# A first chunk with an order of its own, in an mLSTM cell followed by a cosine-gated feed-forward layer

## The chip, the cores and the metric

The kernel runs on one core of a Trainium2 chip. The metric is the device time of one execution in microseconds (us), lower being better. Where several executions of a kernel are timed, their median is given with the lowest and the highest; one further execution was taken with the hardware profiler, and all rows shown come from that one.

The core has five engines, each with its own queue that it works off in order: TensorE (PE in the profile, with its weight loads as PEld), VectorE (DVE), ScalarE (ACT), GpSimd (POOL) and SyncE (SP), which here only issues DMAs. A waiting instruction holds up all that stand behind it in its queue.

## The reference

```python
# q, k, v, o_gate: (4, 8, 768, 40); i_gate, f_gate: (4, 8, 768)
for t in range(S):
    m_new = np.maximum(f[t] + m, i[t])
    f_stab, i_stab = np.exp(f[t] + m - m_new), np.exp(i[t] - m_new)
    m = m_new
    C = f_stab * C + i_stab * outer(v[t], k[t])      # (B, H, 40, 40)
    n = f_stab * n + i_stab * k[t]
    y[t] = sigmoid(o[t]) * (C @ q[t]) / max(abs(n . q[t]), 1)
x = y as (3072, 320)                                 # heads side by side
h = x @ w_in                                         # (3072, 2048)
out = (h * cos(h)) @ w_out                           # (3072, 320)
```

The weights w_in (320 x 2048) and w_out (2048 x 320) arrive as 64-bit floats and are turned into 32-bit floats on the chip.

## The kernel before

**Tiling.** The sequence of 768 is cut into 6 chunks (c) of 128 steps. A chunk of one batch element (b = 0 to 3) with all 8 heads is a cell, n = 4c + b. Within a cell the recurrence is done as matrix products: scores (L490), a decay matrix E that is masked (`decay_exponents`, L396, POOL), exponentiated (`decay`, L410, ACT) and multiplied into the scores (`weigh`, L496, DVE), then values (`values`, L506 to L525, PE) into vt. Between cells the state st[b] is faded (`fade`, L588, POOL), its increment is computed (`seam`, L605) and added (`state`, L627, DVE). `normalize_turned` (L534 to L546) makes x of vt and of the o gate, which `turn_gate` (L468) has turned.

**Two parts beside each other.** While the cells of chunk c + 1 are computed, the feed-forward layer of chunk c runs (`both_parts`, called for each c and b). Its 2048 hidden columns are cut into 16 blocks of 128; a half (c, b, i) handles two of them, f2 = 2b + i. The steps of a half, in the order of data: up-products into two PSUM banks (`Up`, L645 and L651, PE), rounding (`near`, L659, ACT), the remainder (`rest`, L662, DVE), sine (`sin`, L667, ACT), gate (`gate`, L671, DVE), which frees the PSUM bank for the next half's up-products. One half later come the down-products with w_out: in chunk 0 plainly (`down`, L683), in later chunks with 7 products for 8 (`products`, L761), for which POOL makes sums of w_out in chunk 1 (`weight_sums`, L707 to L710). I write 1.0 for b = 1, i = 0 of chunk 0, and round b for its two halves.

**The weights are made in chunk 0.** A piece of w_in (512 columns of one of two row blocks, or the piece of the last 64 rows, w_in_l) or of w_out (two blocks) is loaded as bits by SP, then taken apart on ACT (`take_apart`, two activations, L150 and L152), joined on DVE (`put_together`, L157, L159, L161), and the last addition is done on POOL (L162). `to_float32` is both. Block f of w_in (four hidden blocks) has three pieces; it is needed from half f.0 = (b = f, i = 0) on. Piece p of w_out is needed by the down-products of half p.

**What sets the order.** It is written out by hand: the program's order on each engine is the order of the calls, `first_cells` and then the halves. Loads are issued by SP in the order of their calls too, and wait there until their buffer is free. Tiles come from pools: the bits of w_in from four buffers, those of w_out from three, E from three, G (the decays of the state, multiplied onto q by `scale_q`, L472) from two. `raws` holds q and k as loaded for two cells; `turn_blocks` (L463) turns them for one cell, `low_dimensions` (L455) copies their last 8 columns, and `clear_low` (L448) fills the second pair with zeros before its first use. `warm` (L830) issues products of zeros. `sin_next` loads ACT's table for the sine ahead of need.

In chunk 0, POOL's order in half 0.0 is: qG, the mask of E for cell 5, the two fills of `clear_low`, the addition of w_out's first piece, the end of `normalize_turned`, the four operations of `fade`.

Of the kernel before, what the change touches and what calls it, by code (L numbers as in the profile page):

```python
# [11 lines left out]
FP = mybir.dt.float32  # L12
# [4 lines left out]
OP = mybir.AluOpType  # L17
# [12 lines left out]
def kernel(  # L30
# [153 lines left out]

    tab = const.tile([128, NC, 4, BH], FP, name="tab")
    R = NC - 1
# [91 lines left out]
    def gates_keep(pg, pd):  # L278
        nc.scalar.copy(out=tab[:, 1:NC, 0:2], in_=pg)
        nc.scalar.copy(out=tab[:, 1:R, 3], in_=pd)  # L280

# [174 lines left out]

    def turn_blocks(n):
        m = n // 2 % 2
        qkT[n] = [p1.tile([128, HP, C], FP, name=f"t{i}", tag=f"t{i}") for i in range(2)]
        for i, w in enumerate("qk"):  # L460
            x = 32 + n % 2 * (WR // 2)
            src = raws[w][m][:, x:x + WR // 2].rearrange("q (p a d) -> q p a d", a=C // 32, d=D)
            nc.vector.transpose(out=qkT[n][i].rearrange("q p (t a) -> q p a t", t=32), in_=src[:, :, :, 0:32])  # L463
# [118 lines left out]
    def fade(n):  # L582

        if B <= n < N - B:
            c, b = divmod(n, B)
            for j, r, s, w in halves(n):
                d = tab[r, c, 3, ts(b, H)].rearrange("p (a j) -> p a j", j=2)[:, :, j]
                nc.gpsimd.tensor_tensor(out=s, in0=s, in1=d.unsqueeze(2).to_broadcast([D, HP, w.stop - w.start]), op=OP.mult)  # L588

# [237 lines left out]
    def warm(k, bank=None):  # L827

        for _ in range(k):
            nc.tensor.matmul(bank or pw, nil, nil.unsqueeze(1).to_broadcast([128, HP, 128]), start=True, stop=True)  # L830

    def first_cells():
        nc.vector.memset(nil, 0.0)
# [71 lines left out]
        outs.append((0, weights_out(0)))  # L905
        load_o(1)
        weigh(2)
        decay_exponents(3)
# [13 lines left out]
        pieces.extend(weights_in(1))  # L922
        load_E(B + 1)
        outs.append((1, weights_out(1)))
# [21 lines left out]
        odd_values(B)  # L946
        scale_q(B)

    spot = const.tile([1, 1], FP, name="spot")
# [6 lines left out]
    def next_out():  # L956
        p, piece = outs.pop(0)
        to_float32(*piece)
        if p + 3 < NF // 2:
            outs.append((p + 3, weights_out(p + 3)))  # L960

    def both_parts(c, b):
# [3 lines left out]
        for i in range(2):  # L966
            f2 = 2 * b + i
            up = Up(c, f2, c > 0 and i == 1)
            if cell and i == 0:
                scores(n)  # L970
                if c == 0 and b == 0:

                    warm(8, psum_o())
            if cell and i == 1:
# [6 lines left out]
            if i == 0:  # L981
                if cell:
                    weigh(n)
                    if n + 1 < N:
                        decay_exponents(n + 1)
                    if n == B:
                        clear_low()
                for e in range(2):
                    up.sin(e)
                    up.gate(e)  # L990
                if (c, b) == (0, 0):
                    turn_blocks(n + 1)
                if c > 0:
                    sums(c, f2)
                if c == 1 and b > 0:
                    weight_sums(f2)
                if b == 0 and 0 < c < NC - 1:
                    sigmoid(c + 1)

                if c == 0 and b > 0 and pieces:  # L1000
                    to_float32(*pieces.pop(0))
                if c == 0:
                    next_out()
                if (c, b) == (0, 0):
                    sigmoid(1)
                elif cell and n + 1 < N:
                    decay(n + 1)
            else:
                if pieces:
                    to_float32(*pieces.pop(0))  # L1010
# [5 lines left out]
                if c > 0:  # L1016
                    sums(c, f2)
                if c == 1:
                    weight_sums(f2)
                if n == B + 1:  # L1020
                    low_dimensions(n + 1)
                if (c, b) == (0, 0):
                    decay(n + 1)
                    sin_next()
                while pieces:
                    to_float32(*pieces.pop(0))
                if cell and n + 1 < N:
# [3 lines left out]
            if cell and i == 0:  # L1031
# [12 lines left out]
                if b == B - 2 and c + 2 < NC:  # L1044
                    load_o(c + 2)
                if c == 0 and pieces:
                    to_float32(*pieces.pop(0))
                sin_next()
# [3 lines left out]
            if i == 1:  # L1052
                if c == 0 and b + 2 < B:
                    pieces.extend(weights_in(b + 2))
                    load_two((n + 3) // 2 * 2)
                    load_E(n + 3)
                if cell and n + 1 < N:
                    if (c, b) != (0, 0):
                        turn_blocks(n + 1)
                    scale_q(n + 1)  # L1060
                if c == 0:
                    next_out()

    pieces, outs = [], []
    with tc.manual_schedule():
        first_cells()
        for c in range(NC):
            for b in range(B):
                both_parts(c, b)
        run(made_of[NC - 1], 14)  # L1070
# [33 lines left out]
```

## Time and profile before

| | us |
|---|---|
| median of 3 executions (lowest to highest) | 547.65 (546.9 to 549.5) |
| the profiled execution | 544.86 |
| its span in the profile | 543.0 |
| busy in the span: PE | 516.1 |
| busy: DVE | 423.9 |
| busy: ACT | 283.4 |
| busy: POOL | 262.6 |
| first up-products of chunk 0 to those of chunk 1 (40.1 to 139.1) | 99.0 |

The page gives the busy time of each engine, the span in 40 equal slices, the groups of equal instructions with the idle time ahead of them and what ended it, and the chain of work that ended last. L numbers are lines of the kernel. In a row of a group, the tiles stand as out<-in, then partitions x elements and the type, then how often; behind the bar the busy time in all (us), the mean of one (ns), and the idle time of the engine just ahead of them with its releaser. Rows of the timeline have start and duration in us instead, and merge equal instructions in a row. A row's PE time is that of instructions whose ends are modelled, so that start to start is the better measure. The granted clock is the share of full speed at which TensorE was allowed to run.

### The profile page before, as it was taken

What the parts mean: (1) busy time and instruction counts of PE and PEld (TensorE: products, weight loads), DVE (VectorE), ACT (ScalarE), POOL (GpSimd) and SP (SyncE); (2) the same over time, 40 slices, a digit from 0 to 9 for tenths busy, and PEclk for the clock granted to TensorE, in tenths of its full rate; (3) what the DMA queues carried; (4) which work ended last, traced back from release to release, by engine and by line L of the source; (5) the groups of instructions that cost most, each with busy time, mean ns of one, the idle gap of its engine ahead of it and who ended that gap; (6) DMA issues with size and microseconds to landing.
All of it is one profiled execution on the core that took longest, in us unless ns stands there. A gap on an engine that the chain in (4) does not pass through costs nothing.

```text
span 543.0 us, 10536 instructions
## 1 busy us (share of the span) xinstructions
PE 516.1 (95%) x3842; PEld 349.4 (64%) x3842; DVE 423.9 (78%) x906; ACT 283.4 (52%) x539; POOL 262.6 (48%) x446
## 2 busy tenths in 40 slices
PE   7999498989989999999999999999999999999996
PEld 4884264545556767657767757767757767575756
DVE  5897879997876887887878887887888878664636
ACT  2879767746565537546527546436546533221321
POOL 7542866465467777744553545554424432221211
PEclk9969699999999999999999999999999999999999
DMA  9998997998327539229449319338420000010001
GB/s 136 222 207 199 277 195 227 192 235 172 44 94 166 63 97 193 51 75 185 45 103 179 46 72 198 47 105 174 44 82 18 1 5 6 2 49 1 0 1 48
DMA packets 98051, 57.81 MB, mean 106 GB/s; under 512 B 62336, under 2 KB 90080, under 8 KB 98000
## 3 DMA queue, kind: packets, MB, share of 16 engines
q1 hardware_dynamic: 96528, 55.64, 48.9%
q0 software_dynamic: 1424, 1.49, 1.2%
q8 instruction: 30, 0.49, 0.4%
q14 instruction: 21, 0.17, 0.1%
q10 hardware_dynamic: 48, 0.02, 0.0%
HBM read 51.71 MB, written 4.11 MB: 103 GB/s over the span
## 4 chain that ended last, share of the span: by engine, by line
PE 69%; DVE 11%; ACT 6%; issue 5%; POOL 4%; SPq 3%; DMA 1%; ACTq 0%; DVEq 0%; POOLq 0%
PE pup L645 25%; PE acc L761 23%; PE pup L651 8%; PE po L683 3%; PE late L761 2%; PE ps L490 2%; DVE n L662 2%; PE vt L525 2%; PE vt L516 1%; ACT E L410 1%; DVE g L671 1%; PE pu L605 1%; SPq L327 1%; POOL w_out_sb L162 1%; DVE t L463 1%
## 5 line engine op out<-in xcount | busy, mean ns | idle before, releaser
L645 PE MATMUL pup<-xT,w_in_sb 128*128 128x512 f32 x384 | 176.1, 601 | 5.0 <-DVE g L671 5.0
L659 ACT ACTIVATE n<-pup 128x512 int32<-128x512 f32 x96 | 53.9, 596 | 207.0 <-PE pup L651 146.6
L662 DVE SCALAR_TENSOR_TENSOR n<-pup,n 128x512 f32<-128x512 f32 x96 | 63.2, 687 | 85.1 <-ACT n L659 83.5
L645 PEld LDWEIGHTS pup<-xT,w_in_sb 128*128 128x128 f32 x384 | 69.8, 190 | 91.7 <-issue 78.7
L725 POOL TENSOR_TENSOR D<-g 128x128 f32<-128x128 f32 x40 | 19.6, 490 | 150.1 <-DVE g L671 136.0
L667 ACT ACTIVATE n<-n 128x512 f32<-128x512 f32 x96 | 59.5, 632 | 16.4 <-DVE n L662 16.4
L671 DVE SCALAR_TENSOR_TENSOR g<-pup,n 128x512 f32<-128x512 f32 x96 | 62.2, 685 | 1.8 <-ACT n L667 0.2
L761 PE MATMUL acc<-w_out_sb,g 128*128 128x160 f32 x320 | 58.5, 304 | 0.0
L761 PE MATMUL acc<-T,g 128*128 128x160 f32 x320 | 57.8, 300 | 0.0
L651 PE MATMUL pup<-xT,w_in_l 64*128 64x512 f32 x192 | 54.3, 641 | 0.0
L761 PEld LDWEIGHTS acc<-w_out_sb,g 128*128 128x128 f32 x320 | 47.8, 190 | 5.4 <-issue 3.9
L761 PEld LDWEIGHTS acc<-T,g 128*128 128x128 f32 x320 | 48.2, 190 | 3.1 <-issue 2.7
L410 ACT ACTIVATE E<-E,tab 128x128 f32<-128x128 f32 x160 | 49.1, 391 | 0.3
L683 PE MATMUL po<-w_out_sb,g 128*128 128x320 f32 x128 | 39.5, 465 | 9.0 <-POOL w_out_sb L162 8.9
L683 PEld LDWEIGHTS po<-w_out_sb,g 128*128 128x128 f32 x128 | 25.3, 203 | 23.0 <-POOL w_out_sb L162 10.6
L761 PE MATMUL acc<-T,S 128*128 128x160 f32 x160 | 35.0, 300 | 1.9 <-POOL T L709 1.9
L546 POOL TENSOR_TENSOR yt<-yt,db 128x128 f32<-128x128 f32 x20 | 11.1, 557 | 50.4 <-DVE db L541 50.4
L396 POOL TENSOR_SCALAR_AFFINE_SELECT E<-E 128x1024 f32<-128x1024 f32 x22 | 24.5, 1113 | 19.2 <-DMA E<-M_d 14.5
L490 PEld LDWEIGHTS ps<-t,t 40*128 40x128 f32 x384 | 24.9, 188 | 10.9 <-issue 7.9
L496 DVE TENSOR_TENSOR E<-ps,E 128x512 f32<-128x512 f32 x48 | 30.7, 681 | 0.0
L472 POOL TENSOR_TENSOR qG<-t,G 128x512 f32<-128x512 f32 x20 | 25.4, 1271 | 9.4 <-DVE t L463 9.1
L651 PEld LDWEIGHTS pup<-xT,w_in_l 64*128 64x128 f32 x192 | 14.6, 184 | 23.4 <-issue 19.9
(178 smaller groups left out, 935.1 us busy)
## 6 DMA issues: line engine op xcount, KB each, us to landing
E<-M_d SPq DMA_DIRECT2D x22, 512.0 KB
qr<-in_q_dram SPq DMA_DIRECT2D x36, 160.0 KB
kr<-in_k_dram SPq DMA_DIRECT2D x36, 160.0 KB
G<-G_d SPq DMA_DIRECT2D x20, 256.0 KB
bits<-in_moe_w_out_dram SPq DMA_DIRECT2D x8, 640.0 KB
bits<-in_moe_w_in_dram SPq DMA_DIRECT2D x32, 128.0 KB
out_dram<-o_sb SPq DMA_DIRECT2D x24, 160.0 KB
o<-in_o_gate_dram SPq DMA_DIRECT2D x40, 80.0 KB
```

Source lines behind the costliest of these rows:

```text
L410: nc.scalar.activation(out=Es[n][:, h], in_=Es[n][:, h], func=AF.Exp, scale=-1.0, bias=tab[:, c, 0, g:g + 1])
L472: nc.gpsimd.tensor_tensor(out=qG, in0=qkT[n][0], in1=Gs[n], op=OP.mult)
L490: nc.tensor.matmul(ps[j][:, p], kT[r, p], qT[r, p], start=True, stop=True)
L496: nc.vector.tensor_tensor(out=w, in0=pss[n][j], in1=w, op=OP.mult)
L645: nc.tensor.matmul(pu, w_in_sb[:, i, ts(2 * f2 + e, 128)], x(i), start=(i == 0 and not low_first), stop=(i == NK - 1 and low_first))
L651: nc.tensor.matmul(pu, w_in_l[r, f2], x(NK, r), start=low_first, stop=not low_first)
L659: nc.scalar.activation(out=self.n[e], in_=self.pu[e], func=AF.Copy, bias=0.25)
L662: nc.vector.scalar_tensor_tensor(out=self.n[e].bitcast(FP), in0=self.pu[e], scalar=0.25, in1=self.n[e], op0=OP.add, op1=OP.subtract)
L667: nc.scalar.activation(out=r, in_=r, func=AF.Sin, scale=TWO_PI_DOWN)
L671: nc.vector.scalar_tensor_tensor(out=g, in0=self.pu[e], scalar=TWO_PI, in1=self.n[e].bitcast(FP), op0=OP.mult, op1=OP.mult)
L683: nc.tensor.matmul(po[c][b], gs[c, f][:, ts(b, C)], w_out_sb[:, f], start=(f == 0), stop=(f == NF - 1))
L761: nc.tensor.matmul(a, lhs, rhs, start=start, stop=stop)
```

## The change

Chunk 0 gets a function of its own, `first_parts`, in place of `both_parts`, from which the cases for chunk 0 are taken out. Its order differs from before in these points:

- in half 0.0 the addition of w_out's first piece stands ahead of the mask of E, and `clear_low` has gone to the end of `first_cells`; the second piece of ACT's w_in work stands ahead of the sigmoid;
- in halves 1.1 and 2.1 the gates stand ahead of the join of w_in_l; in 1.0 and 2.0 one join of w_in stands ahead of the gates; POOL adds w_out ahead of qG and of the mask; `turn_blocks` is split in two, with the join of w_out between q and k;
- the take-aparts on ACT are put into other places, most of them ahead of `near` of the next half, and w_in's pieces are loaded one by one (`more`), with the q and k of cells 6 and 7 ahead of the first of them; the load of E for cell 5 is issued ahead of w_in's second block;
- after the first down-products come 20 products of zeros added to the same banks (`hold`);
- `fade` is one operation on all 128 partitions and 384 columns instead of four on 40 partitions, with its factors in a tile of their own (`fades`), filled by two copies on 64 partitions each (`gates_keep`); this holds for all chunks. In chunk 0 it stands ahead of `normalize_turned`.

```diff
-    tab = const.tile([128, NC, 4, BH], FP, name="tab")
+    tab = const.tile([128, NC, 2, BH], FP, name="tab")
+    fades = const.tile([128, NC, BH // 2], FP, name="fades")
...
     def gates_keep(pg, pd):
         nc.scalar.copy(out=tab[:, 1:NC, 0:2], in_=pg)
-        nc.scalar.copy(out=tab[:, 1:R, 3], in_=pd)
+        for j in range(2):
+            r = slice(64 * j, 64 * j + 64)
+            nc.scalar.copy(out=fades[r, 1:R], in_=pd[r].rearrange("q c (g j) -> q c g j", j=2)[:, :, :, j])
...
     def fade(n):
...
-            for j, r, s, w in halves(n):
-                d = tab[r, c, 3, ts(b, H)].rearrange("p (a j) -> p a j", j=2)[:, :, j]
-                nc.gpsimd.tensor_tensor(out=s, in0=s, in1=d.unsqueeze(2).to_broadcast([D, HP, w.stop - w.start]), op=OP.mult)
+            s = st[n % B].rearrange("q (i p w) -> q i p w", i=3, p=HP)
+            d = fades[:, c, ts(b, HP)].unsqueeze(1).unsqueeze(3).to_broadcast([128, 3, HP, 32])
+            nc.gpsimd.tensor_tensor(out=s, in0=s, in1=d, op=OP.mult)
...
+    def hold(k):
+
+        z = nil[:, 0:1].to_broadcast([128, DM])
+        for j in range(k):
+            nc.tensor.matmul(po[0][j % B], nil, z, start=False, stop=False)
...
     def first_cells():
...
         load_o(1)
+        load_E(B + 1)
...
         pieces.extend(weights_in(1))
-        load_E(B + 1)
...
         scale_q(B)
+        clear_low()
...
     def next_out():
         p, piece = outs.pop(0)
-        to_float32(*piece)
+        put_together(*piece)
...
+    feed = []
+
+    def more():
+        for piece in feed[0]:
+            pieces.append(piece)
+            break
+
+    def first_parts(b):
+        n = B + b
+        for i in range(2):
+            f2 = 2 * b + i
+            up = Up(0, f2)
+            if (b, i) == (0, 0):
+                feed.append(piece for f in range(2, NF // 4) for piece in weights_in(f))
+                load_two(n + 2, "qk")
+                more()
+                load_two(n + 2, "Kv")
+            if i == 0:
+                scores(n)
+                if b == 0:
+                    warm(8, psum_o())
+                for e in range(2):
+                    up.near(e)
+                for e in range(2):
+                    up.rest(e)
+                weigh(n)
+                if b > 0:
+                    decay_exponents(n + 1)
+                for e in range(2):
+                    up.sin(e)
+                take_apart(*outs[0][1])
+                if b == 0:
+                    for e in range(2):
+                        up.gate(e)
+                    turn_blocks(n + 1)
+                    next_out()
+                    decay_exponents(n + 1)
+                    take_apart(*pieces[0])
+                    sigmoid(1)
+                else:
+                    if pieces:
+                        put_together(*pieces.pop(0))
+                        more()
+                    for e in range(2):
+                        up.gate(e)
+                    next_out()
+                    decay(n + 1)
+                down_slot(0, f2)
+                turn_gate(n)
+                values(n)
+                seam(n)
+                fade(n)
+                normalize_turned(n)
+                low_out(n)
+                if n == 2 * B - 1:
+                    load_two(n + 3, "qk")
+                if n > B + 1:
+                    load_E(n + 3)
+                if b == B - 2:
+                    load_o(2)
+                sin_next()
+                if b > 0:
+                    if pieces:
+                        take_apart(*pieces[0])
+                        put_together(*pieces.pop(0))
+                        more()
+                        take_apart(*pieces[0])
+                    take_apart(*outs[0][1])
+            else:
+                if n == 2 * B - 1:
+                    load_two(n + 3, "Kv")
+                for e in range(2):
+                    up.near(e)
+                if b == 0:
+                    take_apart(*pieces[1])
+                for e in range(2):
+                    up.rest(e)
+                if b == 0:
+                    for _ in range(2):
+                        put_together(*pieces.pop(0))
+                        more()
+                else:
+                    state(n)
+                for e in range(2):
+                    up.sin(e)
+                    up.gate(e)
+                weigh_k(n + 1)
+                odd_values(n + 1)
+                if b == 0:
+                    take_apart(*pieces[0])
+                    take_apart(*outs[0][1])
+                if pieces:
+                    put_together(*pieces.pop(0))
+                    more()
+                if n == B + 1:
+                    low_dimensions(n + 1)
+                if b == 0:
+                    state(n)
+                    decay(n + 1)
+                    sin_next()
+                else:
+                    turn_blocks(n + 1, (0,))
+                next_out()
+                scale_q(n + 1)
+                if b > 0:
+                    turn_blocks(n + 1, (1,))
+                down_slot(0, f2)
+                if b == 0:
+                    hold(20)
+                if b == 1:
+                    load_two(n + 3)
+                if b < 2:
+                    load_E(n + 3)
+                    take_apart(*pieces[0])
...
     def both_parts(c, b):
...
-            up = Up(c, f2, c > 0 and i == 1)
+            up = Up(c, f2, i == 1)
...
             for b in range(B):
-                both_parts(c, b)
+                if c == 0:
+                    first_parts(b)
+                else:
+                    both_parts(c, b)
```

`turn_blocks(n, which)` turns q, k or both; otherwise it is as before.

More of the change, by code (lines that the diff above doesn't have):

```diff
@@ L455, in low_dimensions, with turn_blocks @@
                 nc.scalar.copy(out=hi[:, :, 0:D - 32], in_=lo[:, :, 32:D])
-    def turn_blocks(n):
+    def turn_blocks(n, which=(0, 1)):
         m = n // 2 % 2
-        qkT[n] = [p1.tile([128, HP, C], FP, name=f"t{i}", tag=f"t{i}") for i in range(2)]
-        for i, w in enumerate("qk"):
+        if n not in qkT:
+            qkT[n] = [p1.tile([128, HP, C], FP, name=f"t{i}", tag=f"t{i}") for i in range(2)]
+        for i in which:
+            w = "qk"[i]
             x = 32 + n % 2 * (WR // 2)
@@ L967, in both_parts @@
             f2 = 2 * b + i
-            up = Up(c, f2, c > 0 and i == 1)
+            up = Up(c, f2, i == 1)
             if cell and i == 0:
                 scores(n)
-                if c == 0 and b == 0:
-                    warm(8, psum_o())
             if cell and i == 1:
@@ L985, in both_parts @@
                         decay_exponents(n + 1)
-                    if n == B:
-                        clear_low()
                 for e in range(2):
@@ L990, in both_parts @@
                     up.gate(e)
[L991 to L994, printed above, removed]
+                sums(c, f2)
                 if c == 1 and b > 0:
                     weight_sums(f2)
-                if b == 0 and 0 < c < NC - 1:
+                if b == 0 and c < NC - 1:
                     sigmoid(c + 1)
[L1000 to L1006, printed above, removed]
+                if cell and n + 1 < N:
                     decay(n + 1)
             else:
-                if pieces:
-                    to_float32(*pieces.pop(0))
                 if cell:
@@ L1015, in both_parts @@
                     up.gate(e)
-                if c > 0:
-                    sums(c, f2)
+                sums(c, f2)
                 if c == 1:
                     weight_sums(f2)
[L1020 to L1026, printed above, removed]
                 if cell and n + 1 < N:
@@ L1045, in both_parts @@
                     load_o(c + 2)
-                if c == 0 and pieces:
-                    to_float32(*pieces.pop(0))
                 sin_next()
@@ L1052, in both_parts @@
             if i == 1:
[L1053 to L1056, printed above, removed]
                 if cell and n + 1 < N:
-                    if (c, b) != (0, 0):
-                        turn_blocks(n + 1)
+                    turn_blocks(n + 1)
                     scale_q(n + 1)
-                if c == 0:
-                    next_out()
     pieces, outs = [], []
```

## Prediction

> **What bounds the kernel now.** I read the page first. TensorE (PE) is busy for 95% of the span, so only stretches where it waits or runs slowly can be won. The group rows show where it waits, the clock row where it was slow (second slot in tenths: 50% to 99% granted).
>
> ```profile
> PEclk9969699999999999999999999999999999999999
> ...
> L645 PE MATMUL pup<-xT,w_in_sb 128*128 128x512 f32 x384 | 176.1, 601 | 5.0 <-DVE g L671 5.0
> ...
> L683 PE MATMUL po<-w_out_sb,g 128*128 128x320 f32 x128 | 39.5, 465 | 9.0 <-POOL w_out_sb L162 8.9
> ```
>
> Next, the timeline of PE, 39 to 165 us: the first chunk with its four rounds (round b, halves b.0 and b.1). The columns are start, us, engine, line, and in brackets the idle time before.
>
> ```profile
> 62.22 7.51 PE L683 MATMUL po<-w_out_sb,g 128*128 128x320 f32 x16 [7.35 <-POOL w_out_sb L162]
> ...
> 75.23 4.57 PE L683 MATMUL po<-w_out_sb,g 128*128 128x320 f32 x16
> ...
> 93.15 3.70 PE L645 MATMUL pup<-xT,w_in_sb 128*128 128x512 f32 x8 [2.02 <-DVE g L671]
> ...
> 99.56 4.57 PE L683 MATMUL po<-w_out_sb,g 128*128 128x320 f32 x16 [0.76 <-POOL w_out_sb L162]
> ```
>
> The first down-product waits 7.35 us and then takes 7.51 instead of 4.57. The windows say why: the granted clock is 1.00 from 42 to 57 us, 0.50 from 58 to 68. Later it waits 2.02 + 0.76, then 1.45 + 0.76 (at 116.92 and 123.33). In all 7.35 + 2.94 + 4.99 = 15.3 us, which is all that the first chunk can give. POOL's timeline shows what holds the first:
>
> ```profile
> 56.49 1.32 POOL L396 TENSOR_SCALAR_AFFINE_SELECT E<-E 128x1024 f32<-128x1024 f32 x1 [12.43 <-DMA E<-M_d]
> 57.76 1.46 POOL L448 MEMSET qr<- 128x1312 f32 x1
> 59.16 1.47 POOL L448 MEMSET kr<- 128x1312 f32 x1
> 60.60 1.56 POOL L162 TENSOR_TENSOR w_out_sb<-w_out_sb,bits 128x640 int32<-128x640 int32 x1
> ```
>
> POOL stood at a mask whose DMA had not landed; the addition stood behind it, though DVE had joined its bits by 53.24. Rounds 1 and 2 have another bound, DVE:
>
> ```profile
> 90.15 1.44 DVE L161 SCALAR_TENSOR_TENSOR w_in_l<-bits,w_in_l 128x256 int32<-128x256 int32 x1
> 91.51 0.86 DVE L627 TENSOR_TENSOR st<-st,pu 40x128 f32<-40x128 f32 x4
> 92.40 1.29 DVE L671 SCALAR_TENSOR_TENSOR g<-pup,n 128x512 f32<-128x512 f32 x2
> ...
> 98.63 1.29 DVE L662 SCALAR_TENSOR_TENSOR n<-pup,n 128x512 f32<-128x512 f32 x2 [0.83 <-ACT n L659]
> ```
>
> From n at 74.89 to n at 98.63 is 23.74 us, with 0.83 us idle. PE's own work in a round is 21.5 (up at 93.15 to up at 116.92, less 2.21 idle). Round 3 has fewer joins; DVE idles 5.2 us there and PE sets the pace.
>
> **The change, part by part**, against the profiled run (544.86, span 543.0), which lies 2.8 under the median 547.65. The difference is put on the median.
>
> *First addition.* Mask and addition change places; the two fills (2.9 us) go right behind qG (ends 44.06), where POOL then idles 12.43, so they cost nothing. The addition starts after the join, 53.24 + 1.56 = 54.8; PE ends its up-products at 54.87. So the down-product runs 54.9 to 59.5. The ceiling is 7.35 + 2.94 = 10.3.
>
> *20 zero products* follow it. Eight of 512 columns took 1.90 (L830), so 320 columns take 0.145 each, 2.9 in all (5.8 at half clock), to 62.4. They are hidden if the next up-products start later, and cost up to 2.9 if not.
>
> *Gates of half 0.1.* ACT does a take-apart (1.23) ahead of the sigmoid, so the o gate is ready at 54.1, 1.2 later; DVE goes on from there for 3.6 and starts n at 57.7 (before: 60.14). Then n 1.2, two joins of 1.55 with about 1 us of blocking, gates from 63.0, and PE's up(1.0) starts at 63.7 instead of 69.57: 5.9 earlier, with 1.3 idle behind the zero products. The mask's load issued ahead of w_in's second block moves that block's landing by 2.2 to 2.7 us (512 KB by the stream's rate), to about the moment when ACT wants it; up to 1.3 us of waiting there is covered by the next item.
>
> *A new wait, and it decides.* ACT now takes apart the next w_in piece before near(1.0) (L659), not after. On SP, the q/k loads (640 KB) are issued ahead of that piece. SP's stream is continuous here: its share of the DMA engines is 0.87 to 1.6 from 57 to 75 us, and adding up the issued bytes against the queue's packets, the G load ends at 65.4. The q/k loads took 3.05 and half a w_in block 2.5, hence 70.9, plus 0.8 to 1.7 until an engine uses it (E issued at 51.93: bytes through at 55.7, POOL starts at 56.49; the E before: 35.6 and 37.27). I take 71.7; ACT needs 1.23; near(1.0) starts at 72.9. Its up-products end at 68.4: ACT is late, and behind it stand n, the weighing, the gates and PE's values. Before, near(1.0) was at 74.26. **The 5.9 shrinks to 1.35**, and the zero products and the late sigmoid are covered by this 4.5 us wait.
>
> *Rounds 1 and 2: gates ahead of joins.* In b.1 the w_in_l join (2.0) goes behind the gates, so up(b+1) need not wait for it; in b.0 a join goes ahead of the gates, where PE still has a down-product and the values to do (4.57 + 2.2 us). DVE does the same operations, so its round falls only by idle time (0.83) and blocking. Blocking: L159 takes 0.49, and 1.47 at 80.53 beside POOL's addition (80.23 to 81.65); such excess sums to 2.77 in round 1 (0.98 + 0.34 + 1.01 + 0.44). Bare, a round is 20.1. Bounds for blocking: 0 to 2.8, or worse by as much again. In the new order the join of w_in_l meets no POOL addition (POOL is through with the previous one and kw by then) and the w_out join starts when POOL's addition ends; I take 0.5, and 0.5 of idle: 21.1 against 23.74, −2.6. In round 2 PE's 21.5 is the floor; kT is now turned behind the w_out join, so scores wait some 0.6: 22.1 against 23.77, −1.7. Round 3: some of its 0.76, −0.3.
>
> [...]
>
> *Fading* is one POOL operation, 128x384, for four (1.38, or 2.1 beside DVE). Not in the trace; bounds 0.78 (384 columns at kw's 1.04 per 512) and 0.95 (at qG's 1.27); I take 0.9, as kw too has a broadcast input. Where PE waits for POOL's weight sums (1.95 at 158.58), the fade stands ahead of them on POOL: −0.5. Elsewhere it is covered by POOL's idle time. The table copy becomes two (0.27 each) ahead of 2.12 us of ACT idle: nothing. Nothing else in the later chunks changes.
>
> Sum: −1.35 − 2.6 − 1.7 − 0.3 − 0.5 = −6.45. 547.65 − 6.45 = **541.2**.
>
> **Rivals.**
>
> *Bits in time* (8%): ACT doesn't wait; 5.9 stays, and all 5.0 us of later waits go, and the 0.5: −11.4, 536.2. For it: nothing but the possibility that the stream runs ahead (331 GB/s from 66 to 68 us). Against it: the byte sum.
>
> *DVE rounds keep their blocking* (26%): only idle goes: −1.35 − 0.8 − 0.8 − 0.3 − 0.5 = −3.75, 543.9. For it: DVE has the same 688 instructions. Against: the w_in_l join has changed neighbours.
>
> *Late bits* (22%), on the other side. If the piece lands at L, n(1.0) comes at L + 1.8, level with before at L = 73. Every us after that costs one, and from L of about 73.2 PE idles over 3.1 us behind the second down-product (ends 74.4; the weighed E comes at L + 4.3), which is how long it idled before the clock fell at 57.95: 10.24 us at half clock, some 3 net. Against 5.1 of later gains the sum is nought at L = 75 and +2.9 at L = 78 (550.6). Against it: 1152 KB would have to take 12 us, 96 KB per us, where no window of the stretch shows under 165. For it: SP's queue is in order, and one wait for a buffer would do. 13% end within 0.5%, 9% beyond.
>
> [...]
>
> That the change doesn't do what it says has under 1%: the addition's only other input is the join at 53.24.
>
> **How the numbers follow.** Forecast 44%: 541.2. Faster by over 0.5% (2.7 us, about what a measurement can tell from no change): 44 + 8 + 26 = 78%; same 13%; slower 9%. The range runs from the first rival to inside the third, 536 to 547: it leaves out the slower part and some of the same.
>
> **What would show it.** Right: the first down-product at about 55 without idle time, and 4.6 long; granted clock 1.00 from 58 to 68; near(1.0) on ACT at about 73 right behind a take-apart that follows idle time; up(2.0) near 89; up(3.0) near 111; the next chunk's up near 133; fade rows of about 0.9. Wrong: near(1.0) at 69 (first rival) or past 76 (third); n to n in round 1 still over 23 us (second); half clock anywhere between 60 and 90; fade rows over 1.4.

## The result, and the profile after

The changed kernel takes 539.89 us in the median of 4 executions (537.57 to 541.19), the kernel before 547.27 (546.87 to 549.5, 4 executions): a ratio of 0.9852, 95% interval 0.9808 to 0.9896, or 7.4 us less between the medians where 6.45 were forecast (541.2). (The ratios here and below are estimated from all executions; they are not the quotients of the medians.) The profiled execution took 541.19 with a span of 539.4; that of before 544.86 with 543.0. These two spans differ by 3.6 only, and the stages say where the rest is:

| us | start to first up-products | half 0.0 | round 1 | round 2 | round 3 | rest | span |
|---|---|---|---|---|---|---|---|
| before | 40.09 | 29.48 | 23.58 | 23.77 | 22.15 | 403.93 | 543.0 |
| after | 46.62 | 24.12 | 22.51 | 21.44 | 21.56 | 403.15 | 539.4 |

The boundaries are the starts of the up-products of halves 0.0, 1.0, 2.0, 3.0 and of the next chunk (here "half 0.0" is all of round 0, halves 0.0 and 0.1). Ahead of its first up-products, in cells that the change hardly touches, after lost 6.53 us; from there on it won 10.1. The clock row of the page, with the two group rows that carried the prediction, for after:

```profile
PEclk9587999999999999999999999999999999999999
...
L650 PE MATMUL pup<-xT,w_in_sb 128*128 128x512 f32 x384 | 176.3, 602 | 3.1 <-DVE g L676 3.0
...
L688 PE MATMUL po<-w_out_sb,g 128*128 128x320 f32 x128 | 36.6, 439 | 1.3 <-POOL w_out_sb L162 1.3
```

Down-products waited 9.0 and wait 1.3; up-products waited 5.0 and wait 3.1. The low clock has moved: before, slots 3 and 5 (27 to 41 and 54 to 68 us) were low; now slots 2 to 4 (13.5 to 54) are, and none behind them.

The timeline of PE in the first chunk of after (start, us, engine, line, tiles, idle time ahead):

```profile
61.87 4.58 PE L688 MATMUL po<-w_out_sb,g 128*128 128x320 f32 x16 [0.15 <-POOL w_out_sb L162]
66.28 2.92 PE L841 MATMUL po<-nil 128*128 128x320 bf16 x20
...
70.74 3.67 PE L650 MATMUL pup<-xT,w_in_sb 128*128 128x512 f32 x8 [1.55 <-DVE g L676]
...
77.51 4.57 PE L688 MATMUL po<-w_out_sb,g 128*128 128x320 f32 x16 [1.15 <-POOL w_out_sb L162]
...
93.25 3.60 PE L650 MATMUL pup<-xT,w_in_sb 128*128 128x512 f32 x8
...
98.95 4.57 PE L688 MATMUL po<-w_out_sb,g 128*128 128x320 f32 x16
```

The first down-product waits 0.15 in place of 7.35 and takes 4.58 in place of 7.51; the zero products are 2.92 long; 1.55 is left ahead of up(1.0), the 2.02 ahead of up(2.0) is gone. POOL shows why (same columns):

```profile
60.25 1.56 POOL L162 TENSOR_TENSOR w_out_sb<-w_out_sb,bits 128x640 int32<-128x640 int32 x1 [8.17 <-issue]
61.76 1.10 POOL L399 TENSOR_SCALAR_AFFINE_SELECT E<-E 128x1024 f32<-128x1024 f32 x1
62.82 0.83 POOL L593 TENSOR_TENSOR st<-st,fades 128x384 f32<-128x384 f32 x1
```

The addition now comes first, then the mask, and the fade is one row of 0.83. What the prediction called decisive isn't there. ACT, after:

```profile
73.80 0.66 ACT L150 ACTIVATE w_in_sb<-bits 128x512 f32<-128x512 f32 x1
...
75.50 1.09 ACT L664 ACTIVATE n<-pup 128x512 int32<-128x512 f32 x2 [0.47 <-PE pup L656]
```

The take-apart ahead of near(1.0) has no idle time before it, so its bits were there, and near(1.0) waits for PE.

### The profile page after: what moved, and what is told of

Same layout as the page of the kernel before. It is cut to its first block, busy times and chain, and to the rows that moved or that the text cites. A ratio compares the mean times of both kernels' runs of the same rounds, so it can differ in the third digit from the quotient of the medians.

```text
span 539.4 us, 10523 instructions
## 1 busy us (share of the span) xinstructions
PE 522.1 (97%) x3862; PEld 354.8 (66%) x3862; DVE 417.6 (77%) x906; ACT 284.0 (53%) x540; POOL 251.5 (47%) x398
## 4 chain that ended last, share of the span: by engine, by line
PE 82%; ACT 8%; DVE 6%; issue 2%; POOL 1%; DMA 0%; ACTq 0%; DVEq 0%
PE pup L650 28%; PE acc L766 23%; PE pup L656 8%; PE po L688 6%; PE ps L495 4%; PE late L766 2%; PE vt L530 2%; ACT E L413 2%; PE vt L521 2%; PE ph L511 1%; PE pu L610 1%; PE pt L445 1%; DVE n L667 1%; PE pw L835 1%; ACT L413 1%
## 5 line engine op out<-in xcount | busy, mean ns | idle before, releaser
L688 PE MATMUL po<-w_out_sb,g 128*128 128x320 f32 x128 | 36.6, 439 | 1.3 <-POOL w_out_sb L162 1.3
L495 PEld LDWEIGHTS ps<-t,t 40*128 40x128 f32 x384 | 26.1, 196 | 11.5 <-issue 7.7
L688 PEld LDWEIGHTS po<-w_out_sb,g 128*128 128x128 f32 x128 | 23.7, 190 | 13.8 <-POOL w_out_sb L162 2.3
L656 PEld LDWEIGHTS pup<-xT,w_in_l 64*128 64x128 f32 x192 | 14.6, 184 | 23.4 <-issue 21.4
L766 PEld LDWEIGHTS acc<-T,S 128*128 128x128 f32 x160 | 26.2, 190 | 4.3 <-issue 2.7
L766 PE MATMUL acc<-w_out_sb,S 128*128 128x160 f32 x160 | 28.7, 299 | 0.0
```

What stands on the lines that cost most here:

```text
L495: nc.tensor.matmul(ps[j][:, p], kT[r, p], qT[r, p], start=True, stop=True)
L656: nc.tensor.matmul(pu, w_in_l[r, f2], x(NK, r), start=low_first, stop=not low_first)
L688: nc.tensor.matmul(po[c][b], gs[c, f][:, ts(b, C)], w_out_sb[:, f], start=(f == 0), stop=(f == NF - 1))
L766: nc.tensor.matmul(a, lhs, rhs, start=start, stop=stop)
```

## The experiments

Two theories were to be told apart first. *The prediction's*: the addition gives most of it back to a wait of ACT for bits, and DVE's order gains the rest. *The rival*: that wait isn't there, and each edit pays for itself. Once the first cells had come out at two lengths for no reason in the code, a third question came up: what draws that length.

**The changed kernel again** (e1). No edit.

> The changed kernel as it is, profiled a second time. In its first profile the stretch from chunk 0's first up-products to the end took 492.8 us (before: 502.9), but the first cells ahead of it took 46.6 us (before: 40.1), with the granted clock at half from 13.9 us on. Theory: the clock's half stretch in the first cells is a lottery of its windows, not the change's; this profile then has its own pattern of half-clock stretches ahead of 48 us, and the stretch behind the first up-products is again 490 to 497 us. Rival 1: the change slows the first cells; then the first up-products are again at 46 to 47 us, with a drop at about 14 us. Rival 2 (as predicted): with quick first cells (up-products at about 40 us) ACT waits 3 to 4.5 us for the bits ahead of the near step of half 1.0, and the stretch behind is 494 to 498 us. Time: 537 to 542 us.

Measured: 538.04 (537.57 to 541.23), ratio 0.9837 (0.979 to 0.9883) to before on that chip, 548.82. Its profile has first cells of 41.42 in place of 46.62, with the same program; rounds 1 to 3 repeat to 0.03 (22.50, 21.41, 21.57), the rest to 0.02 (403.17). So the later stages can be read from one profile, the first cells can't. From its first up-products to its end, e1 is 1.6 slower than the first profile (494.38 and 492.78), all of it in half 0.0 (25.73): its clock is low from 32.44 to 46.09, 4.7 us into that stage, and the first up-products take 5.99 where those at full clock take 3.70. PE, e1:

```profile
41.42 5.99 PE L650 MATMUL pup<-xT,w_in_sb 128*128 128x512 f32 x8
...
53.37 3.70 PE L650 MATMUL pup<-xT,w_in_sb 128*128 128x512 f32 x8
...
67.15 3.67 PE L650 MATMUL pup<-xT,w_in_sb 128*128 128x512 f32 x8 [1.53 <-DVE g L676]
```

ACT waits for the bits ahead of near(1.0) by next to nothing there:

```profile
70.50 0.68 ACT L150 ACTIVATE w_in_sb<-bits 128x512 f32<-128x512 f32 x1 [0.23 <-DMA bits<-in_moe_w_in_dram]
...
71.91 1.08 ACT L664 ACTIVATE n<-pup 128x512 int32<-128x512 f32 x2
```

**Without the zero products** (e2; the products that add nothing to the result are left out).

```diff
                 down_slot(0, f2)
-                if b == 0:
-                    hold(20)
```

> The changed kernel without the 20 products of zeros. Theory: PE then idles about 4.5 us between the first down-product and the up-products of half 1.0, and the clock can fall for 10.24 us as it did before at 57.95, which costs 3 to 5 us: 541 to 545 us where it falls, and unchanged within 0.5 us where the window's place lets it through. Rival: the zero products only cover idle time and the clock stays (gap too short); then the same time within 0.3%, 538 to 541 us.

Measured: 542.14 (537.99 to 543.14), ratio 0.9881 (0.9837 to 0.9925), 4.1 above e1 on the same chip. First cells 46.91, like after's. From there to the end 494.39 against 492.78, so the zero products are worth 1.6 in profiles that are alike. The timeline of PE, e2, and the window of the low clock (length, then busy us with counts for PE, PEld, DVE, ACT, POOL, the granted clock, the DMA share, GB/s):

```profile
71.23 6.06 PE L650 MATMUL pup<-xT,w_in_sb 128*128 128x512 f32 x8 [4.30 <-DVE g L676]
```

```profile
69.20:76.00 6.80, 4.77 (x6) 2.17 (x7) 6.58 (x14) 6.23 (x13) 3.59 (x5) 0.50 1.23 213
```

Without them PE idles 4.30 and the clock is at 0.50 for 6.8 us, and the up-products take 6.06 in place of 3.67. They need no cover: they stand in idle time.

**near ahead of the next piece** (e3): in rounds 1 and 2 the take-apart goes behind `near`, `rest` and `weigh`, where no wait for bits can hold up near.

```diff
                 weigh(n)
+                if 0 < b < 3:
+                    take_apart(*pieces[0])
...
                     load_E(n + 3)
-                    take_apart(*pieces[0])
```

> The changed kernel with the take-aparts of the next w_in piece moved behind the near step in halves 1.0 and 2.0, which is where ACT could be held by bits that have not landed. Theory (from the first profile, where ACT did not wait): no change, within 0.3% of the changed kernel. Rival (the prediction's decisive wait): in executions with quick first cells ACT waits up to 4.5 us there, so this kernel is 2 to 4 us faster in the median, 535.5 to 538 us.

Measured: 538.31 (537.76 to 541.87), ratio 0.983 (0.9788 to 0.9871): no change from e1's 538.04 that could be told. Taking the take-apart from before near, where I had seen the decisive wait, shows no gain. In the profile there was none to be had: near(1.0) waits 4.44 for PE there. That profile drew first cells of 40.04, the shortest of all, and shows the bits late in another place: at w_in's second block, ahead of the sigmoid, which I had put down as covered. ACT, DVE and PE of e3:

```profile
52.11 0.68 ACT L150 ACTIVATE w_in_sb<-bits 128x512 f32<-128x512 f32 x1 [1.93 <-DMA bits<-in_moe_w_in_dram]
```

```profile
56.18 0.88 DVE L473 STREAM_TRANSPOSE oT<-og 128x384 f32<-128x384 f32 x1 [3.00 <-ACT og L323]
```

```profile
65.92 6.47 PE L650 MATMUL pup<-xT,w_in_sb 128*128 128x512 f32 x8 [3.66 <-DVE g L676]
```

Bits, 1.93; the gate behind them on ACT, 3.00 on DVE; the gates of half 0.1 behind those, 3.66 on PE, and up-products of 6.47 at half clock (64.72 to 71.55). Quick first cells lose here a part of what they won. Rounds 1 and 2 are 24.09 and 22.15, longer than after's 22.51 and 21.44; the slow up-products are 2.8 of the first.

**The addition alone** (e4): before, with the fills in `first_cells` and the mask behind the addition, nothing else.

```diff
         scale_q(B)
+        clear_low()
...
                     weigh(n)
-                    if n + 1 < N:
+                    if n + 1 < N and n > B:
                         decay_exponents(n + 1)
-                    if n == B:
-                        clear_low()
...
                 if (c, b) == (0, 0):
+                    decay_exponents(n + 1)
                     sigmoid(1)
```

> The kernel before with one part alone: the first addition of w_out ahead of the mask, and the two fills at the end of the first cells; no zero products, old order of gates and joins, four fades. Theory: the first down-product starts without its wait of 7.35 us; the up-products of half 1.0 wait for the gates of half 0.1 instead, so 3 to 6 us are won there, less a clock drop if PE idles over 3 us; the rounds behind keep 23.6 us each: 541.5 to 544.5 us. Rival: the wait moves whole to the near step or the gates, nothing won: 546 to 549 us. If the first cells' length is a lottery, its profile shows either pattern; if the rival on the first cells holds, its up-products start at 40 us.

Measured: 546.43 (543.61 to 548.63, 12 executions), ratio 0.9957 (0.9927 to 0.9986): 2.4 of the 10.8 us between the medians of e1 and of before on this chip, and less than the 3 to 6 us expected. PE, e4:

```profile
60.45 4.58 PE L683 MATMUL po<-w_out_sb,g 128*128 128x320 f32 x16
...
69.53 6.14 PE L645 MATMUL pup<-xT,w_in_sb 128*128 128x512 f32 x8 [4.51 <-DVE g L671]
```

The first wait is gone, and PE idles 4.51 right behind the down-product instead, at the gates of half 0.1; the clock falls from 67.67 to 74.50. Rounds 2 and 3 and the rest stay as before (23.77, 22.14, 403.87). So the addition alone pays little: the next gap takes most of it back.

**Four operations for the fade** (e5): the change with the old `fade`, `tab` and copy.

```diff
-            s = st[n % B].rearrange("q (i p w) -> q i p w", i=3, p=HP)
-            d = fades[:, c, ts(b, HP)].unsqueeze(1).unsqueeze(3).to_broadcast([128, 3, HP, 32])
-            nc.gpsimd.tensor_tensor(out=s, in0=s, in1=d, op=OP.mult)
+            for j, r, s, w in halves(n):
+                d = tab[r, c, 3, ts(b, H)].rearrange("p (a j) -> p a j", j=2)[:, :, j]
+                nc.gpsimd.tensor_tensor(out=s, in0=s, in1=d.unsqueeze(2).to_broadcast([D, HP, w.stop - w.start]), op=OP.mult)
```

> The changed kernel with the four fading operations of before (and one table copy). Theory: chunk 0 in itself changes little (rounds 21.4 to 23 us); the stretch from chunk 1's up-products to the end, 403.2 us in four profiles with the single operation and 403.9 in two with four, goes back to 403.9: 0.7 us lost, 538.5 to 541 us. Rival: POOL's four operations block DVE's joins again, and rounds 1 and 2 go up by 1 us each: then 540.5 to 543 us.

Measured: 540.49 (540.21 to 542.37), ratio 0.9874 (0.9823 to 0.9924); before on that chip 548.0. The median lies 2.4 above e1, from another chip and with the first cells' lottery in it. The stages are sharper: rounds 1 to 3 as in after (22.53, 21.45, 21.55), and the rest 403.97, where after has 403.15. The rest is 403.83 to 403.97 in the four profiles with four operations (before twice, e4, e5), and 403.06 to 403.20 in the nine with one: 0.8 between the means.

**Joins ahead of gates** (e6): the old order of gates and w_in's joins in rounds 1 and 2 (for round 3 no piece of w_in is left).

```diff
                 else:
+                    for e in range(2):
+                        up.gate(e)
                     if pieces:
                         put_together(*pieces.pop(0))
                         more()
-                    for e in range(2):
-                        up.gate(e)
...
                 else:
+                    if pieces:
+                        put_together(*pieces.pop(0))
+                        more()
                     state(n)
...
-                if pieces:
+                if pieces and b == 0:
                     put_together(*pieces.pop(0))
```

> The changed kernel with the joins of w_in in rounds 1 and 2 back in their old places (w_in_l ahead of the gates in 1.1 and 2.1, the other behind the gates in 1.0 and 2.0); all else as changed. Theory (gates ahead of joins make the rounds short): rounds 1 and 2 take 23.4 to 23.8 us again instead of 22.5 and 21.4, so 3 us are lost, 541 to 543 us. Rival: the rounds became short since POOL's operations no longer meet DVE's joins or since bits come sooner, whatever the order of gates and joins: rounds of 21.5 to 22.5 us, 538 to 540 us.

Measured: 541.82 (538.94 to 542.58), ratio 0.9876 (0.9826 to 0.9925). Its profile has the first cells and the half 0.0 of after (46.66 and 24.13), so the two can be laid over each other: from the first up-products to the end 494.04 against 492.78. Round 1 is 22.71 against 22.51, round 2 22.78 against 21.44, round 3 21.33 against 21.56. The order is worth 1.3, nearly all in round 2, where 3 were expected: the rounds stay well below the 23.58 and 23.77 of before. The rows of PE say what the rest is. Before's waits for POOL's addition in rounds 2 and 3 (0.76 each) and its 2.02 ahead of up(2.0) are gone in after and in e6 alike, and a wait of 1.15 for the addition in round 1 is new in both. DVE, POOL and PE of e6:

```profile
104.62 1.48 DVE L159 TENSOR_SCALAR w_out_sb<-w_out_sb 128x640 int32<-128x640 int32 x1
```

```profile
104.32 1.42 POOL L162 TENSOR_TENSOR w_in_sb<-w_in_sb,bits 128x512 int32<-128x512 int32 x1 [3.57 <-DVE w_in_sb L161]
```

```profile
116.28 1.98 PE L650 MATMUL pup<-xT,w_in_sb 128*128 128x512 f32 x4 [1.30 <-DVE g L676]
```

DVE's L159 starts 0.30 after POOL's addition and ends 0.36 after it, 1.48 long instead of some 0.5; PE then waits 1.30 for the gates.

**Bits sooner** (e7): the load of E back behind w_in's second block, and the sigmoid ahead of the take-apart, so that neither the bits nor the take-apart stands ahead of the o gate.

```diff
         load_o(1)
-        load_E(B + 1)
...
         pieces.extend(weights_in(1))
+        load_E(B + 1)
...
                     decay_exponents(n + 1)
-                    take_apart(*pieces[0])
                     sigmoid(1)
+                    take_apart(*pieces[0])
```

> The changed kernel with the load of E for cell 5 back behind w_in's second block, and the sigmoid back ahead of the take-apart in half 0.0. In a profile with quick first cells (40.0 us) ACT waited 1.93 us for those bits ahead of the sigmoid, and PE's up-products of half 1.0 waited 3.66 us for the gates. Theory: in such executions up to 3 us are won, in those with slow first cells about 1 us (the take-apart no longer delays the o gate): median 535.5 to 538 us. Rival: the stream of loads sets the pace anyway, the wait goes on to the next piece's bits: 537.5 to 540 us, and the profile shows ACT waiting for bits ahead of the near step of half 1.0.

Measured: 538.08 (536.79 to 540.58), ratio 0.9822 (0.9774 to 0.987). First cells 41.54 as in e1's 41.42, half 0.0 24.82 against 25.73, with the clock low to the same point (46.01 and 46.09). The gap ahead of up(1.0) shrinks from 1.53 to 0.76. PE, e7:

```profile
66.36 3.67 PE L650 MATMUL pup<-xT,w_in_sb 128*128 128x512 f32 x8 [0.76 <-DVE g L676]
```

What has gone from ahead of the sigmoid is the take-apart, 1.24 of ACT (53.37 to 54.61 in e1). The medians can't tell e7 from e1.

**Warm first cells** (e8): e7 with more zero products in the first cells (2 + 4 + 1 more), to see whether the length of the first cells follows PE's activity.

```diff
+        warm(2)
...
+        warm(4)
...
-        warm(1)
+        warm(2)
```

> As the run before, with seven more products of zeros in the first cells (2 at about 12 us, 4 and 1 at about 29 us), where all profiles so far show a fall of the clock to half for 10 us or more at 30 to 38 us, and three of six an earlier one at 14 to 20 us. Theory: the falls come from too little work of PE in a window and are rarer with the zeros: first up-products at 37 to 41 us in every execution, spread of times halved, median 533 to 536 us. Rival: the falls stay (the zeros are too few), and the zeros cost up to 1.7 us: 537 to 540 us.

Measured: 538.54 (536.74 to 541.44), ratio 0.9832 (0.9783 to 0.988). Its profile has no fall of the clock ahead of 35 us, and every execution a mean granted clock of 0.990 to 0.993, where e1's six had 0.978 to 0.989. Yet the median is that of e7, and the expected 533 to 536 was missed. The profile shows a loss, on ACT:

```profile
73.56 0.68 ACT L150 ACTIVATE w_in_sb<-bits 128x512 f32<-128x512 f32 x1 [3.85 <-DMA bits<-in_moe_w_in_dram]
...
74.70 1.07 ACT L664 ACTIVATE n<-pup 128x512 int32<-128x512 f32 x2
```

This is the wait of the prediction: bits late by 3.85, near(1.0) behind them at 74.70. Rounds 1 and 2 become 24.08 and 22.28, 1.57 and 0.84 more than e7's. An early PE doesn't explain it: up(1.0) starts at 66.57 here and at 66.36 in e7, where ACT waits 0.26 for the same bits. The loads do: SP issues the piece 3.4 later. SP in e7, then in e8:

```profile
60.39 4.12 SPq L139 DMA_DIRECT2D bits<-in_moe_w_in_dram  x4
```

```profile
63.83 4.44 SPq L139 DMA_DIRECT2D bits<-in_moe_w_in_dram  x4
```

What held SP's stream back in e8 was not followed further.

**The piece ahead of q and k** (e9): e8, with the next w_in piece issued ahead of the q/k loads.

```diff
-                load_two(n + 2, "qk")
                 more()
-                load_two(n + 2, "Kv")
+                load_two(n + 2)
```

> The kernel of the run e8 (load of E behind w_in's second block, sigmoid ahead of the take-apart, seven more products of zeros in the first cells) with the first piece of w_in's third block issued on SP ahead of the q and k of cells 6 and 7. In e8 ACT waited 3.85 us for this piece ahead of the near step of half 1.0, and the round behind took 24.1 instead of 22.5 us. Theory (the stream of loads holds the near step whenever the first cells are quick, as the prediction had it): the piece lands some 3 us sooner, the wait goes to under 1 us, the near step comes at about 71 us, and 2 to 3.5 us are won on e8: median 535 to 536.5 us. Rival: the wait goes on to the next loads in the queue (q and k of cells 6 and 7, or w_in's next pieces), and the time stays at 537.5 to 539.5 us.

Measured: 536.38 (535.77 to 537.91), ratio 0.9798 (0.9752 to 0.9844), the lowest median of all. Rounds 1 and 2 are 22.51 and 21.43 again. ACT, e9:

```profile
69.80 0.67 ACT L150 ACTIVATE w_in_sb<-bits 128x512 f32<-128x512 f32 x1
...
71.52 1.08 ACT L664 ACTIVATE n<-pup 128x512 int32<-128x512 f32 x2 [0.48 <-PE pup L656]
```

The wait of 3.85 is gone, and near(1.0) waits for PE, 3.2 earlier. Rounds 1 and 2 are 2.4 shorter than e8's; between the medians it is 2.2, from two chips and with intervals that overlap. That SP's order did it is not shown by these profiles. SP issued the piece at 56.72 in place of 63.83, but of these 7.1 us only 3.0 are the loads of q and k that stood ahead of it in e8 (60.88 to 63.83); the loads before them came 4.2 sooner in this execution (a load of E at 54.98 and 59.14). And e7, in the old order, has rounds of 22.51 and 21.44 too.

**The same without the warm products** (e10): e7 with the edit of e9.

> As the run before, without the seven products of zeros in the first cells. Theory: where the first cells are slow, the piece was in time anyway, where they are quick, as before: between e7 (538.1 us) and e9: 536 to 538 us, with a wider spread than e9 by the clock's falls ahead of 30 us. Rival: the zeros don't matter, the same as e9 within 0.5 us.

Measured: 537.07 (535.5 to 540.38), ratio 0.9814 (0.9769 to 0.986). The profile drew slow first cells (46.61). The spread of the times is 4.9 us, e9's 2.1. The difference of the medians, 0.7, isn't told by these intervals; the edit of e9 shows no clear gain here. The difference of the spreads fits the clock: e10's profile falls at 13.91, e9's only at 35.76.

**Before, again** (e11). No edit; one execution.

> The kernel before, profiled a second time. Theory (the first cells' length is a lottery of the clock, which both kernels draw): its first up-products start anywhere from 40 to 47 us, its rounds take about 29 (or less, where slow first cells let the loads come in time: 24 to 27), 23.6, 23.8 and 22.1 us, the stretch from chunk 1's up-products to the end 403.9 us. Rival: the kernel before always has quick first cells: 40 us again.

Measured: 550.89, span 549.0. First cells 46.60, half 0.0 26.02, round 1 26.67, round 2 23.74, round 3 22.14, rest 403.83. The kernel before has both lengths of first cells too. The windows from 14 to 18 us, for the profile of before shown with the prediction, for e11 and for after (columns as above):

```profile
14.00:18.00 4.00, 4.00 (x40) 3.58 (x36) 3.36 (x5) 3.97 (x5) 2.08 (x4) 1.00 0.99 255
```

```profile
14.00:18.00 4.00, 4.00 (x25) 3.40 (x23) 2.86 (x4) 3.22 (x5) 1.99 (x4) 0.50 0.98 289
```

```profile
14.00:18.00 4.00, 4.00 (x25) 3.40 (x23) 2.88 (x4) 3.24 (x5) 1.97 (x4) 0.50 0.98 257
```

PE is recorded as busy throughout in all three; with the clock at 1.00 it does 40 products, at 0.50 it does 25. And e11's wait at POOL was not the 7.35 of the first profile. POOL and PE, e11:

```profile
56.71 1.09 POOL L396 TENSOR_SCALAR_AFFINE_SELECT E<-E 128x1024 f32<-128x1024 f32 x1 [6.92 <-DMA E<-M_d]
```

```profile
63.56 4.58 PE L683 MATMUL po<-w_out_sb,g 128*128 128x320 f32 x16 [1.88 <-POOL w_out_sb L162]
...
72.62 6.70 PE L645 MATMUL pup<-xT,w_in_sb 128*128 128x512 f32 x8 [4.49 <-DVE g L671]
```

E's load doesn't depend on PE: it landed at the same time (56.49 and 56.71), while PE came 6.5 later, so the wait is 1.88. The gap of 4.49 at the gates and a clock fall from 71.90 to 78.73 stand in its place.

## Why the prediction was right, and where it was wrong

Each pair is of profiles with first cells of about the same length. The stages are parted here where the forecast parted them, at n(1.0) and n(2.0), DVE's starts of `rest` in halves 1.0 and 2.0:

| us | first up-products to n(1.0) | to n(2.0) | to up(3.0) | round 3 | rest | sum |
|---|---|---|---|---|---|---|
| forecast | −1.35 | −2.6 | −1.7 | −0.3 | −0.5 | −6.45 |
| slow cells: after less e11 | −4.94 | −1.22 | −2.20 | −0.58 | −0.68 | −9.6 |
| quick cells: e1 less before | −3.68 | −1.25 | −2.26 | −0.58 | −0.76 | −8.5 |

The slow pair is alike up to the first up-products (46.62 and 46.60, the clock low to 48.04 and 48.01). The quick pair is so only roughly: e1's clock is low to 46.09, before's to 40.88.

- **First addition and zero products: right.** The wait goes, the down-product takes 4.58, and 2.92 of zero products lie in idle time; e4 shows the term alone, e2 its second half. That PE would then be late at the gates of half 0.1 was in the prediction; that without the zero products the clock falls there (e2 4.30 of idle time, e4 4.51) was not.
- **"A new wait, and it decides … The 5.9 shrinks to 1.35": the step that failed.** It set a date on SP against a date on PE, and put 4.5 us of waiting at near(1.0). That wait is not there: near(1.0) waits for PE in after (0.47), and in e1, where ACT waits 0.23 for the bits, it starts 4.76 behind up(1.0) as in after. SP's date was about right: 71.7 for the bits, and 69.78 in e7, 70.50 in e1, 73.56 in e8. PE's was too early: 63.7 for up(1.0) came from a profile with first cells of 40.09 and full clock behind them. In e3, which drew such first cells (40.04) and differs from after only in what follows, up(1.0) is at 65.92, held by the bits of w_in's second block. In e1 the start is 1.33 later than in before, and the low clock adds 1.9 to the first up-products (5.99 for 4.06): 63.7 + 3.3 = 67.0, measured 67.15. In after PE began at 46.62 and got to up(1.0) at 70.74, 24.12 on, where 23.6 were forecast. The mechanism exists, as e8 shows (3.85, near(1.0) 8.13 behind up(1.0)), but there the bits were late and PE no earlier than in e7. In no profile of the kernel as changed does it decide.
- **The "up to 1.3 us" at w_in's second block, "covered": wrong with the quickest first cells.** In e3 it is 1.93 and passes on to PE as 3.66, with a fall of the clock; in e1 the same take-apart, at 53.37, has no idle time ahead of it. Nothing covered the 3.66, since the 4.5 that were to do that are not there.
- **Round 1, −2.6: mis-sized.** Blocking did not go to 0.5. DVE and POOL of after:

```profile
79.01 1.20 DVE L159 TENSOR_SCALAR w_in_sb<-w_in_sb 128x512 int32<-128x512 int32 x1
```

```profile
78.64 1.29 POOL L399 TENSOR_SCALAR_AFFINE_SELECT E<-E 128x1024 f32<-128x1024 f32 x1
```

The join that went ahead of the gates met POOL's mask: +0.77, with 0.19 and 0.27 at 82.05 and 87.65, 1.2 in all. From n to n round 1 is 22.5 (76.13 to 98.63, 0.92 idle), 21.1 forecast; against the 23.74 of the profile that I worked from it is −1.24, and the slow pair has −1.22. The order of joins itself is worth 0.2 here (e6).
- **Round 2, −1.7: right in kind, 0.6 short.** PE's own 21.5 is the floor, and 21.4 is what came; the 0.6 that scores were to wait for kT isn't seen. e6 gives 1.34 of it back, and the wait of 0.76 for POOL's addition is gone in e6 too.
- **Round 3 and the fade: right, small.** −0.58 for −0.3. The fade is 0.82 (822 to 835 ns) for 0.9, and the rest of the kernel 0.8 shorter for 0.5: the wait for the weight sums falls from 1.95 to 1.36, and where the other 0.2 came from wasn't looked for.

```profile
L766 PE MATMUL acc<-T,S 128*128 128x160 f32 x160 | 35.0, 300 | 1.4 <-POOL T L714 1.4
```

- **The sum came near because of errors that cancel, and by luck.** The stretch to n(1.0) was forecast 2.3 to 3.6 too small, since 4.5 us of waiting were taken off that aren't there; round 1 was forecast 1.4 too large; the rest together 1.0 too small. Pairs of profiles give 8.5 and 9.6, and the medians 7.4 from four executions each and 10.8 on e1's chip: all lie above the 6.45, and that the first of them lies so near is a matter of which executions were drawn. The profile stood for a quick draw of the first cells, and I took its 7.35 and its clock fall for what every execution has.

In the first chunk, gaps of PE of 1.55 (after) and 2.02 (before) left the clock at 1.00; gaps of 3.66 (e3), 4.30 (e2), 4.49 (e11), 4.51 (e4) and 7.35 (before) each hold a fall to 0.50. The fall came 2.46 (e3), 2.28 (e2), 3.77 (e11), 2.65 (e4) and 3.08 (before) after PE stopped, so the 3.1 that the rival on late bits counted with is one value of several. The fall at 13.9 us in after has no such gap ahead of it: PE is recorded as busy from 6 us on there (4.00 of 4.00 from 6 to 10, 3.50 of 3.50 from 10.4 to 13.9).

What draws the length of the first cells can be narrowed down from the 13 profiles. The clock is low from 30.64 to 40.88 and from 57.95 to 68.19 in before, from 13.91 to 27.56 and from 37.81 to 48.04 in after: lengths of 10.24 and 13.65, with 17.07 and 10.24 between them, all whole multiples of 3.41. The same spacing is in e3, whose falls at 30.59 and 64.72 are 34.13 apart (ten times), and in e11, where 23.89 lie between the end at 48.01 and the fall at 71.90 (seven times). The time of the first fall, less the largest multiple of 3.413 (a third of 10.24) in it, is called its offset here. It differs from execution to execution, and the first cells go with it, in both kernels alike:

| offset, us | profiles | first fall | first cells |
|---|---|---|---|
| 0.2 to 0.9 | after, e2, e6, e10, e11 | 13.9 to 14.6 | 46.6 to 46.9 |
| 1.2 to 1.7 | e1, e7, e8, e9 | 32.4 to 35.8 | 41.4 to 42.3 |
| 2.7 to 2.8 | e4, e5 | 19.7 to 19.9 | 44.6 to 44.7 |
| 3.3 | before, e3 | 30.6 | 40.0 to 40.1 |

So the change did not lengthen the first cells; after drew another offset than before. That the offset is the cause fits all 13, and is argued: no run sets it.

Open: what makes the clock fall at these places, with PE recorded as busy. The seven zero products of e8 and e9 go with a higher clock (0.989 to 0.993 in the mean of all 12 executions, 0.976 to 0.990 in the 18 of e1, e7 and e10), but in the profiles they did not shorten the first cells: e7 and e9 have the same offset (1.63), the fall moves from 32.35 to 35.76, both end at 46.0, and the first cells take 41.54 and 42.32. A stretch of low clock that begins between 30.59 and 38.49 us is in all 13 profiles, and no experiment removed it. That the clock goes by windows (the theories of e1 and e2), or by too little work of PE in one (e8), is not shown: the runs give the times of the falls and their spacing, not what causes them.

## What to carry to other kernels

A gain at one wait is worth what the next gap leaves of it: the addition alone gave 2.4 us on a chip where the whole change gave 10.8, and the zero products in the gap behind it were worth 1.6. Where a stage's length is a draw, take a second profile of the kernel before, and compare stages of like draws, from the points at which the forecast counted; a step that needs a date on one engine against a date on another needs both dates in each draw. A piece of work that stands on an engine ahead of a step that needs nothing of it can hand its own wait on to that step: the take-apart ahead of near(1.0) waited 0.26 in e7, with near at 71.12, and 3.85 in e8, with near at 74.70, though up(1.0) started at 66.36 and 66.57.

## What the runs showed of the hardware that I had not expected

- The granted clock fell to 0.50 in stretches of 6.83 (e4, 67.67 to 74.50), 10.24 (before, 30.64 to 40.88) or 13.65 us (after, 13.91 to 27.56), two, three or four times 3.41, though PE was recorded as busy for most of each (4.97 of 6.80, 10.04 of 10.24, 13.65 of 13.65). In before and after all starts and ends of these stretches in the first 100 us lie whole multiples of 3.41 apart.
- It fell between 13.9 and 14.6 us in five profiles (after, e2, e6, e10, e11), though PE is recorded as busy for all of 6 to 13.9 us in after and e11, as it is in before and e9, where it did not fall then; the first cells take 46.6 to 46.9 with that fall, and 40.0 to 42.3 in the six without a fall ahead of 30 us.
- In after, 20 products of zeros (2.92 us) stood ahead of a gap of 1.55, and the clock was 1.00 from 62 to 76 us; in e2, without them, PE idled 4.30, and it was 0.50 from 69.2 to 76.
- DVE's L159 took 0.43 (w_in, 78.94 in before) and 0.49 (w_out, median in before), but 1.47 from 80.53 in before beside POOL's addition (L162, 80.23 to 81.65), 1.48 from 104.62 in e6 beside another (104.32 to 105.74), and 1.20 from 79.01 in after beside the mask (L399, 78.64 to 79.93): it ended 0.35, 0.36 and 0.28 behind POOL. Beside a fill (L448 in before, 57.76 to 59.22) it took 1.37 from 58.13, where L161 beside the next fill (59.16 to 60.63) took 0.69, as at 87.69; and beside the fade (L588, 86.80 to 88.90) L159 took 0.51 from 87.15.
